# One kernel in two stages on one Trainium2 core: a written order table in place of a list scheduler

## The chip, the cores and the metric

The kernel runs on one core of a Trainium2 chip. A core has five engines with instruction streams of their own: TensorE (PE, matmuls; its weight loads are counted as PEld), VectorE (DVE), ScalarE (ACT), GpSimd (POOL) and SyncE (SP), which here issues nearly all DMA transfers. They wait for one another by semaphores. The metric is the time of one execution on the device in microseconds (us), lower is better; the time before is the median of three runs. The profile's span, from the first to the last instruction, is a little shorter than that time.

## The reference

Two stages follow each other. The first is a gated linear attention of 4 batches, 8 heads, 768 steps and head size 48. The second is a gated MLP with a spatial product over the 768 steps (width 384, inner width 1024).

```python
for t in range(S):
    state = alpha[:, :, t, :, None] * state + np.einsum('bhd,bhe->bhde', k[:, :, t], v[:, :, t])
    y[:, :, t] = np.einsum('bhd,bhde->bhe', q[:, :, t], state)
# x = y with the heads side by side: (4, 768, 384)
h = np.maximum(x @ w_in, 0.0)
u, v = h[..., :512], h[..., 512:]
v_n = (v - mean(v)) / np.sqrt(var(v) + 1e-06)          # over the 512
v_s = np.einsum('ts,bsd->btd', w_spatial, v_n) + b_spatial[None, :, None]
out = (u * v_s) @ w_out
```

## The kernel before

The recurrence is done in 24 chunks of 128 steps (6 for each batch). Of a chunk the kernel forms running sums of log alpha by a matmul (`cum`), scales k by exp(-sum) and q by exp(sum) (`kt`, `qt`), transposes both on TensorE (`trk` or `tr`) and copies them out (`ev`), forms masked scores (`sc`, then `m` with a mask) and from them and the state of the chunk before the output (`y`). The state is carried on by `upd` (matmul), `z` (add), `S` (scale) and `sb` (a bf16 copy). Then `y` is copied and transposed (`xs`, `xt`, `xe`) into x. The first six chunks go as three pairs, in which each partition holds two neighbouring steps, so that the pieces of a load are twice as long (384 bytes); their operations have a p in the name (`cump`, `ktp`). The second stage has for each batch six groups of `v` with statistics (`bn`, `rs`, `vn`), eight of `u`, eight of the spatial product `s` with its bias and gate (`g`), and six of the output product `o` with its store (`st`).

Each operation is recorded with its engine or engines, a length in us, what it depends on, and a function that emits it. Nothing is emitted where it is recorded:

```python
class Op:
    def __init__(self, eng, dur, emit, deps=(), prio=0.0, take=None, lat=0.13, cols=0): ...
# ... (cut)
def dma(key, us, emit, deps, prio, eng="SP", issue=0.99, lat=1.9):
    o = op(key + ("issue",), eng, issue, emit, deps, prio=prio)
    return op(key, "DMA", us, lambda _: None, [o], prio=prio, lat=lat)
# ... (cut)
op(("cump", j, par), "PE", 0.33 + 0.1, cum, got(("lnp", j)), prio=P + 2, take=sl_c[par], cols=768)
op(("ktp", j, par), {"POOL": 0.9, "DVE": 0.6}, None, ktf, got(("einvp", j, par), ("kc", 2 * j)) + tr_users("k", jo), prio=P + 4)
```

A list scheduler then runs through the recorded operations while the program is built. It takes the operation that can start first on its engine in a model of time (lengths as given, a load lands 1.9 us or, for single chunks, 3.5 us after its modelled transfer), bent by tables of patience by kind and of nudges for single operations. Where TensorE would wait in the model before 40 us, it puts in junk matmuls, which write a buffer that is not yet in use:

```python
for eng, dur in op.eng.items():
    start = max(ready, free.get(eng, 0.0))
    key = (round(start + (0.5 * dur if len(op.eng) > 1 else 0.0) + op.wait + ..., 2), ...)
    if best is None or key < best[0]:
        best = (key, n, eng, start, dur)
# ... (cut)
if op.take and start < warm_to:            # junk, warm_from 2.0, warm_to 40.0
    # ... (cut) as many junk matmuls of 96 to 384 columns as fit before start
    fill.append(cols)
# ... (cut)
op.emit(eng)
```

Other rules are that a weight load follows a named load of q, k or v (`late`), and that the stores of the first 11 output tiles follow the last loads. The finished program is a fixed stream for each engine; what an engine waits for at run time is found from the data.

Of the kernel before, what the change touches and what calls it, by code (L numbers as in the profile page):

```python
# [16 lines left out]
class Op:  # L17


    def __init__(self, eng, dur, emit, deps=(), prio=0.0, take=None, lat=0.13, cols=0):  # L20
        self.eng = {eng: dur} if isinstance(eng, str) else dict(eng)
        self.emit, self.prio, self.lat, self.cols = emit, prio, lat, cols
        self.take = [take] if isinstance(take, Slot) else list(take or ())
        self.deps = [d for d in deps if d is not None]
        assert not any(isinstance(d, list) for d in self.deps)
        self.end = None
        self.wait = 0.0
        self.big = False


class Ring:


    def __init__(self, bufs):
        self.bufs, self.taken = bufs, []

    def free_at(self, k):

        n = len(self.taken) - self.bufs + k
        if n < 0:  # L40
            return 0.0
        users = self.taken[n].users
        if any(u.end is None for u in users):
            return None
        return max([u.end + u.lat for u in users], default=0.0)
# [7 lines left out]
class Clock:  # L53


    TICK, ENOUGH = 3.4133, 3100.0

    def __init__(self):
        self.count = {}

    def warm(self, t):
        return self.count.get(int(t / self.TICK) - 1, 0.0) >= self.ENOUGH

    def run(self, t, dur, cols):

        end = t + dur * (1.0 if self.warm(t) else 2.0)
        x = t
        while x < end - 1e-9:
            k = int(x / self.TICK + 1e-9)
            y = min(end, (k + 1) * self.TICK)  # L70
            self.count[k] = self.count.get(k, 0.0) + cols * (y - x) / (end - t)
            x = y
        return end


PATIENCE = {"ev": -0.3, "kt": -0.2, "be": 0.2, "sb": -0.1, "bb": 0.3, "ln": 0.2, "z": -0.1, "S": 0.1, "o": 0.2, "cast": -0.1, "rs": 0.1, "trk": -0.1, "xs": -0.3, "xe": -0.2, "y": -0.2, "eexp": -0.3}
# [11 lines left out]
NUDGE = {  # L88
    ("vn", 0, 4): -0.3,
    ("v", 0, 5): 0.6,  # L90
    ("vbp", 0, 0): -0.6,
    ("ev", "q", 1, 1): 0.15,
    ("cast", "w_in", 0, 1): -0.15,
    ("vb", 21): -0.15,
    ("o", 3, 2, "mm", 0): 0.3,
    ("sc", 1, 0): -0.3,
    ("tr", "k", 0, 1): -0.3,
    ("y", 2): 0.15,
    ("ebc", 2): 0.6,
    ("sb", 4): 0.3,  # L100
    ("m", 1, 1, 0): -0.3,
    ("tr", "k", 1, 0): -0.6,
    ("einv", 17): 0.15,
    ("st", 2, 1): 1,
    ("eexp", 10): -0.3,
    ("wt", 5): -0.15,
    ("cast", "w_out", 3): -0.15,
    ("cump", 0, 0): 1,
    ("ev", "q", 0, 1): -0.6,
    ("ln", 7): 0.6,  # L110
    ("cump", 0, 1): 1,
    ("ev", "q", 1, 0): -0.3,
    ("v", 0, 1, "mm", 0): 0.3,
    ("kc", 2): -0.15,
    ("cast", "w_in", 1, 0): 0.6,
    ("wt", 2): -0.15,
    ("u", 0, 3, 1): 1,
    ("ebc", 1): -0.6,
    ("cast", "w_in", 0, 0): -0.15,
    ("eexpp", 1, 1): 0.15,  # L120
    ("st", 1, 4): 1,
    ("cast", "w_in", 0, 2): 0.3,
    ("xt", 3): 0.15,
    ("z", 1): -0.6,
    ("u", 3, 0, 0): -0.3,
    ("lnp", 0): 1,
    ("xs", 7): 0.3,
    ("y", 0): -0.3,
    ("u", 3, 1, 0): -1.5,
}  # L130
PAIRS = (0, 1, 2)
LATE = 3.5
BETWEEN = 0.06
ACT_STATS = ((2, 2), (1, 4))
PIECES = {
    "w_in": ((0, "vc", 1, 0.35), (0, "kc", 2, 0.15)),
    "w_sp": ((0, "vc", 4, 0.35), (0, "qc", 6, 0.25), (0, "qc", 6, 0.25)),
    "w_out": (0, "vc", 7, 0.35),
}


def schedule(ops, fill, warm_from, warm_to):

    free = {}
    clock = Clock()
    small = 0.0
    todo = list(ops)
    while todo:
        best = None
        for n, op in enumerate(todo):  # L150
            if any(d.end is None for d in op.deps):
                continue
            ready = max([d.end + d.lat for d in op.deps], default=0.0)
            waits = [slot.ring.free_at(k) for k, slot in enumerate(op.take)]
            if None in waits:
                continue
            ready = max([ready] + waits)
            for eng, dur in op.eng.items():
                start = max(ready, free.get(eng, 0.0))
                key = (round(start + (0.5 * dur if len(op.eng) > 1 else 0.0) + op.wait + (small if eng == "PE" and not op.big and start < free.get("PE", 0.0) + 0.05 else 0.0), 2),  # L160
                       ready if eng == "DMA" else op.prio)
                if best is None or key < best[0]:
                    best = (key, n, eng, start, dur)
        assert best is not None, "nothing can start"
        _, n, eng, start, dur = best
        op = todo.pop(n)
        if eng == "PE":
            if op.take and start < warm_to:
                t = max([free.get(eng, 0.0), warm_from] + [slot.ring.free_at(k) for k, slot in enumerate(op.take)])
                while True:  # L170
                    each = 0.00042 if clock.warm(t) else 0.00084
                    cols = min(384, int((start - t) / each) // 32 * 32)
                    if cols < 96:
                        break
                    fill.append(cols)
                    t = clock.run(t, 0.00042 * cols, cols)
            end = clock.run(start, dur + (0.0 if op.big or start > free.get(eng, 0.0) + 0.05 else small), op.cols)
            small = 0.0 if op.big else BETWEEN
        else:
            end = start + dur  # L180
        for slot in op.take:
            slot.ring.taken.append(slot)
        free[eng] = end
        op.end = end
        op.emit(eng)


@with_exitstack
def kernel(
# [14 lines left out]
    B, H, S, D = q.shape  # L204
# [11 lines left out]
    N = B * NCH  # L216
    WARM = 40.0
# [4 lines left out]
    WK = 3  # L222
    NB, NKP = 3, 2
    LD, LP, WT, ST = 1.03, 1.46, 2.35, 0.8
# [116 lines left out]
    def op(key, *args, **kw):  # L341

        users = kw.pop("use", ())
        o = Op(*args, **kw)
        for s in users:
            s.users.append(o)
        ops.append(o)
        made[key] = o
        o.wait = PATIENCE.get(key[0], 0.0) + NUDGE.get(key, 0.0)
        return o  # L350

    def got(*keys):
        return [made.get(x) for x in keys]
# [42 lines left out]
    def finish_x(i):  # L396
# [20 lines left out]
        def xe(eng):  # L417
            if c == 0:
                tiles(b)
# [20 lines left out]
    def pair(j):  # L440
# [33 lines left out]
        for par in range(2):  # L474
# [45 lines left out]
            op(("ktp", j, par), {"POOL": 0.9, "DVE": 0.6}, None, ktf, got(("einvp", j, par), ("kc", 2 * j)) + tr_users("k", jo), prio=P + 4)  # L520
# [7 lines left out]
            op(("qtp", j, par), "DVE", 0.47, qtf, got(("eexpp", j, par), ("qc", 2 * j)) + tr_users("q", jo), prio=P + 4, use=[sl_c[par]])  # L528
# [111 lines left out]
    def first(i):  # L640
# [16 lines left out]
        dma(("ac", i), LD, load("ac", alpha), io_users("ln", j), P, lat=LATE)  # L657
        dma(("kc", i), LD, load("kc", k), io_users("kt", j), P + 0.1, lat=LATE)
        dma(("qc", i), LD, load("qc", q), io_users("qt", j), P + 0.2, lat=LATE)
        dma(("vc", i), LD, load("vc", v), io_users("vb", j), P + 0.3, lat=LATE)  # L660

# [104 lines left out]
        for s, sl in ((0, sl0), (1, sl1)):  # L766
            op(("m", i, s), "DVE", 0.6, mk(s), got(("sc", i), ("y", i - WK)), prio=P + 7.5, use=[sl])
# [77 lines left out]
    def bias():  # L845
        for th in range(2):
# [9 lines left out]
            op(("bb", th), "PE", 0.2, emit, got(("b_sp",)), prio=50.0, take=sl)  # L856
# [4 lines left out]
    def second_v(b, tt):  # L861
# [51 lines left out]
        op(("rs", b, t0), "ACT", 0.45, rs, got(("bn", b, t0), ("bn", b, tt), ("mv", b, t0)), prio=6.0)  # L913
# [82 lines left out]
    def second_o(b, tt):  # L996
# [31 lines left out]
        if n < KEEP:  # L1028
            late.extend((made[("st", b, tt, "issue")], (x, N - 1, "issue")) for x in ("ac", "kc", "qc", "vc"))
# [9 lines left out]
        (("w_in", half), PIECES["w_in"][1 - half], w_in_sb[half],  # L1039
         moe_w_in.rearrange("(ks p) f -> p ks f", p=128)[:, :, half * DH:half * DH + DH]) for half in (1, 0)]  # L1040
    pieces += [
        (("w_sp", n), PIECES["w_sp"][n], None,
         moe_w_spatial.rearrange("(tt p) s -> p tt s", p=128)[:, 2 * n:2 * n + 2, :]) for n in range(3)]
    pieces += [(("w_out",), PIECES["w_out"], w_out_sb, moe_w_out.rearrange("(ds p) m -> p ds m", p=128))]
    late, fetched, casts = [], [], []

    def fetch(key, after, to, src):
# [9 lines left out]
        dma(key, WT, load, list(fetched[-NRAW] if len(fetched) >= NRAW else []), 10.0 * after[2] + after[3], issue=0.68)  # L1057
        late.append((made[key + ("issue",)], after[1:3] + ("issue",)))
        for j in range(n):
            tt = 2 * key[-1] + j if to is None else None  # L1060

            def cast(eng, j=j, tt=tt):
# [5 lines left out]
               None, cast, got(key), prio=10.0 * after[2] + 12)  # L1068
# [8 lines left out]
    late.append((made[("b_sp", "issue")], ("vc", 0)))  # L1077
# [22 lines left out]
    for o, after in late:  # L1100
        o.deps += got(after)
    for o, tt in casts:
        o.deps += [made[("wt", tt - NROW)]] if tt >= NROW else []
    schedule(ops, fill, 2.0, WARM)
# [30 lines left out]
```

## Time and profile before

| | |
|---|---|
| time, median of 3 runs | 154.69 us (154.53 to 154.72) |
| span of the profile | 152.9 us |
| ScalarE busy | 108.7 us |
| GpSimd busy | 86.0 us |
| HBM read, written | 23.60 MB, 4.72 MB |
| mean granted TensorE clock | 0.995 of full |

The page gives busy time and share of the span for each engine, and the span in 40 equal slices with a digit for the busy tenths of each. Its groups of instructions name a line of the kernel, engine, operation and tiles (out<-in); a line may be that of a helper, as L826 for all matmuls of the second stage and L249 for junk. The chain of waits follows the end of the program back to what released each step. A timeline row has the start, the length, engine, line, operation, tiles and shapes, and in brackets the idle time before it and what ended it. Ends of matmuls are modelled and overlap the next one, so that the distance of starts tells more of TensorE's pace than the length of a row.

### The profile page before, as it was taken

How to read it: one execution, taken by the hardware profiler on the slowest of the kernel's cores; microseconds unless marked ns; L12 is line 12 of the kernel's file. 1: busy time of each engine (PE TensorE's matmuls, PEld its weight loads, DVE VectorE, ACT ScalarE, POOL GpSimd, SP SyncE). 2: the span in 40 equal slices, each digit the busy share in tenths (PEclk: the TensorE clock that was granted, in tenths of full speed). 3: DMA queues.
4: the chain of work that ended last, by engine and by line, in shares of the span. 5: the costliest groups of instructions: out<-in, count | busy, mean ns of one | idle time of the engine just before them, and what ended most of it. 6: DMA issues, size and time to landing. Idle time of an engine off the chain costs nothing.

```text
span 152.9 us, 4478 instructions
## 1 busy us (share of the span) xinstructions
PE 145.2 (95%) x1713; PEld 90.3 (59%) x1713; DVE 121.6 (80%) x260; ACT 108.7 (71%) x268; POOL 86.0 (56%) x151
## 2 busy tenths in 40 slices
PE   6899999799999999999999999999999999999990
PEld 3366756467566666466657556666666565656550
DVE  7888598797899899878799889689789867566820
ACT  3566677697697975899984598998956778880050
POOL 6847356462249698814369987242699873003620
PEclk9999999999999999999999999999999999999998
DMA  4999999799899997998998999999980131230044
GB/s 123 266 313 290 316 242 273 200 285 210 155 296 174 249 205 154 204 221 164 211 209 174 202 190 194 212 184 202 303 322 9 51 107 51 100 110 0 0 157 154
DMA packets 93013, 28.60 MB, mean 187 GB/s; under 512 B 87872, under 2 KB 91456, under 8 KB 92992
## 3 DMA queue, kind: packets, MB, share of 16 engines
q1 hardware_dynamic: 92960, 28.32, 78.9%
q8 instruction: 13, 0.21, 0.6%
q14 instruction: 8, 0.07, 0.2%
q0 software_dynamic: 32, 0.00, 0.0%
HBM read 23.60 MB, written 4.72 MB: 185 GB/s over the span
## 4 chain that ended last, share of the span: by engine, by line
PE 88%; ACT 3%; DVE 3%; DMA 2%; issue 1%; DVEq 0%; ACTq 0%
PE ps L826 52%; PE pt L722 5%; PE pt L752 4%; PE y L413 3%; DMA ac<-in_alpha_dram 2%; PE y L780 2%; PE cum L671 2%; PE tp L738 2%; PE y L623 2%; PE y L774 2%; PE y L249 2%; PE ps L545 2%; PE ps L480 1%; PE ps L836 1%; PE ps L249 1%; PE tp L576 1%
## 5 line engine op out<-in xcount | busy, mean ns | idle before, releaser
L826 PE MATMUL ps<-w_spT,vn 128*128 128x384 bf16 x192 | 37.2, 326 | 0.0
L979 POOL TENSOR_TENSOR gT<-vsb,uT 128x384 bf16<-128x384 f32 x29 | 26.3, 926 | 14.7 <-DVE vsb L966 14.7
L763 DVE TENSOR_TENSOR ptm<-pt,mask 128x512 bf16<-128x512 f32 x36 | 23.3, 680 | 3.2 <-PE pt L752 3.1
L695 POOL TENSOR_TENSOR kt<-kc,binv 128x384 bf16<-128x384 f32 x18 | 16.4, 913 | 12.0 <-ACT binv L683 10.5
L384 POOL TENSOR_TENSOR state<-state,bc 128x192 f32<-128x192 f32 x20 | 10.2, 509 | 22.8 <-DVE state L379 11.6
L826 PEld LDWEIGHTS <-vn 128*128 128x128 bf16 x192 | 16.4, 97 | 8.9 <-issue 0.2
L826 PE MATMUL ps<-w_in,xT 128*128 128x512 bf16 x72 | 19.5, 380 | 0.0
L826 PE MATMUL ps<-xT,w_in 128*128 128x384 bf16 x96 | 18.9, 326 | 0.0
L826 PE MATMUL ps<-w_out_sb,gT 128*128 128x384 bf16 x96 | 18.8, 327 | 0.0
L966 DVE TENSOR_TENSOR vsb<-ps,bsp_bc 128x384 f32<-128x384 f32 x31 | 16.4, 552 | 2.9 <-PE ps L826 2.9
L257 ACT CAST x_sb<-y 128x384 bf16<-128x384 f32 x24 | 11.5, 478 | 9.2 <-PE y L780 5.8
L888 DVE BATCH_NORM_STATS2 stats<-v_sb 128x6 f32<-128x512 bf16 x20 | 13.8, 688 | 2.4 <-ACT v_sb L263 2.3
L263 ACT ACTIVATE v_sb<-ps 128x512 bf16<-128x512 f32 x20 | 11.9, 597 | 3.3 <-PE ps L826 3.1
L259 POOL CAST sbd<-state 64x192 bf16<-64x192 f32 x38 | 13.0, 343 | 1.7
L683 ACT ACTIVATE binv<-cum 128x384 bf16<-128x384 f32 x18 | 8.8, 491 | 6.3 <-PE cum L674 5.7
L259 DVE COPY kqT<-pt 128x1024 bf16<-128x1024 bf16 x15 | 10.3, 690 | 3.3 <-PE pt L722 3.0
L257 ACT COPY xT<-y 128x384 bf16<-128x384 bf16 x24 | 11.4, 480 | 1.8 <-PE y L413 1.4
L263 ACT ACTIVATE uT<-ps 128x384 bf16<-128x384 f32 x24 | 11.2, 492 | 1.0 <-PE ps L826 1.0
L826 PEld LDWEIGHTS <-w_in 128*128 128x128 bf16 x96 | 8.3, 97 | 5.3
L826 PEld LDWEIGHTS <-gT 128*128 128x128 bf16 x96 | 8.4, 98 | 4.9
L918 DVE TENSOR_SCALAR vn<-v_sb,mvs,rstd 128x512 bf16<-128x512 bf16 x24 | 10.3, 467 | 1.1 <-ACT rstd L911 1.1
L257 ACT COPY o_sb<-ps 128x384 f32<-128x384 f32 x9 | 4.3, 481 | 9.1 <-PE ps L826 9.1
(129 smaller groups left out, 296.7 us busy)
## 6 DMA issues: line engine op xcount, KB each, us to landing
ac<-in_alpha_dram SPq DMA_DIRECT2D x18, 192.0 KB, 4.2
kc<-in_k_dram SPq DMA_DIRECT2D x18, 192.0 KB, 4.1
qc<-in_q_dram SPq DMA_DIRECT2D x18, 192.0 KB, 3.8
vc<-in_v_dram SPq DMA_DIRECT2D x18, 192.0 KB, 4.0
raw_w<-in_moe_w_spatial_dram SPq DMA_DIRECT2D x3, 768.0 KB, 5.5
out_dram<-raw_w SPq DMA_DIRECT2D x12, 192.0 KB, 3.1
out_dram<-o_sb SPq DMA_DIRECT2D x9, 192.0 KB, 1.9
raw_w<-in_moe_w_in_dram SPq DMA_DIRECT2D x2, 768.0 KB, 8.1
```

Source lines behind the costliest of these rows:

```text
L257: nc.scalar.copy(out=out, in_=in_)
L259: ENG[eng].tensor_copy(out=out, in_=in_)
L263: nc.scalar.activation(out=out, in_=in_, func=AF.Relu)
L384: ENG[eng].tensor_tensor(out=st["state"], in0=st["state"], in1=st["bc"][:, :, None].to_broadcast([128, HP, D]), op=ALU.mult)
L683: nc.scalar.activation(out=st["binv"], in_=st["cv"], func=AF.Exp, scale=-1.0)
L695: ENG[eng].tensor_mul(out=kt[:, :, :, 0:D], in0=quad(st["kc"]), in1=st["binv"])
L763: nc.vector.tensor_tensor(out=st["ptm"][:, s], in0=st[f"pt{s}"], in1=mask4, op=ALU.mult)
L826: return lambda ps: nc.tensor.matmul(out=out(ps), lhsT=lhsT(), rhs=rhs(), start=start, stop=stop)
L888: nc.vector.bn_stats(out=stats, in_=d["v_sb"][:, tt, :])
L918: nc.vector.tensor_scalar(out=d["vn"][:, t, :], in0=d["v_sb"][:, t, :], scalar1=d["mvs"][:, t, 0:1], scalar2=d["rstd"][:, t:t + 1], op0=AL ...
L966: nc.vector.tensor_tensor(out=hold["vs"], in0=ps[:, 0:TH], in1=bsp_bc[:, th, :], op=ALU.add)
L979: ENG[eng].tensor_tensor(out=bt[b]["gT"][:, dsl, cols], in0=hold["vs"], in1=bt[b]["uT"][:, dsl, cols], op=ALU.mult)
```

## The change

The scheduler, the tables of patience and nudges, the model of the clock and the rules for weight loads and stores go. In their place stands a table with one word for each of the 1108 operations, in the order of emission: a letter for the engine (P TensorE, D VectorE, A ScalarE, G GpSimd, S SyncE, Q the transfer itself), the number of the operation as recorded, and for TensorE the columns of junk matmuls ahead of it. Its purpose is an order that was planned outside the kernel, with the times at which loads really arrived in two traces, and with junk that keeps TensorE going until the first sums.

```diff
-def schedule(ops, fill, warm_from, warm_to):
-    ... (cut: the list scheduler)
+PLAN = """
+G32 Q33 G0 S34 S36 Q35 S38 S96 S40 Q37 S98 D1 S100 S166 A42 Q39 S102 D2 S170
+P43:384:384:384:384:384:384:384:384:384:384:384:384 S168 G3 Q97 S4 P54:384 A46 A44 S172 A45 S303 G47 A57 A55 D48 Q41
+S9 A56 D58 P50:384:384:384:384:384:384:384:96 P52 A51 D59 P61:128 Q99 D53 A62 P63:256 D64 A104 P245:384 P243 P73
+... (cut: 47 more lines of this kind)
+"""
+def replay(ops, fill, plan):
+    for word in plan.split():
+        number, *junk = word[1:].split(":")
+        op, eng = ops[int(number)], LETTERS[word[0]]
+        assert eng in op.eng and not op.done and all(d.done for d in op.deps), op.key
+        fill.extend(int(x) for x in junk)
+        op.emit(eng)
+        op.done = True
...
-    schedule(ops, fill, 2.0, WARM)
+    replay(ops, fill, PLAN)
```

In the first lines G32 is the load of b_sp, G0 the constants, S34, S36, S38 and S40 the loads of log-decay, k, q and v of the first pair, P43 and P54 its two running sums, and P50 its first transposes; S4 and S9 are the two halves of w_in. Where the engine of an operation is free, the table chooses too; this moves some operations:

| operation | engine | before | table |
|---|---|---|---|
| u | VectorE, ScalarE | 8, 24 | 14, 18 |
| ev | VectorE, ScalarE | 26, 4 | 21, 9 |
| ktp | VectorE, GpSimd | 3, 3 | 1, 5 |
| casts of weights | VectorE, ScalarE, GpSimd | 2, 6, 8 | 6, 3, 7 |

Single copies of other kinds (be, sb, g, we, vb, vbp) move by one or two. The matmuls of the two stages are the same in number and shape. Stores stand among the last loads in SyncE's stream. Some dependencies on constants (`cz`) that followed from the model's order before are now written out.

## The prediction

> **What bounds the kernel now.** I read the page first, then busy time by stretches of 10 us, then the chain of waits, then TensorE's timeline, and last the issue and landing of each load. The page:
>
> ```profile
> span 152.9 us, 4478 instructions
> ...
> PE 145.2 (95%) x1713; PEld 90.3 (59%) x1713; DVE 121.6 (80%) x260; ACT 108.7 (71%) x268; POOL 86.0 (56%) x151
> ...
> PE   6899999799999999999999999999999999999990
> ...
> DMA  4999999799899997998998999999980131230044
> ```
>
> TensorE is busy in every slice, and the DMA engines until slice 29 (110 us). But busy TensorE includes junk matmuls, which fill waits to keep the clock up. The stretches of junk alone (columns: length, PE busy, PEld busy, DVE busy, clock, DMA share, GB/s):
>
> ```profile
> 5.48:10.00 4.52, 1.93 (x11) 0.91 (x12) 0.00 (x0) 1.00 1.27 268
> 10.00:20.00 10.00, 4.00 (x24) 1.87 (x22) 0.00 (x0) 1.00 1.16 308
> 20.00:30.00 10.00, 1.89 (x13) 0.99 (x13) 0.00 (x0) 1.00 0.98 249
> 30.00:40.00 10.00, 1.26 (x6) 0.55 (x6) 0.00 (x0) 1.00 0.91 211
> ```
>
> So the slack lies before 40 us. After that TensorE does real work only. The chain of waits, its start and its end:
>
> ```profile
> 0.74 3.76 DMA ac<-in_alpha_dram
> 4.59 0.85 ACT la L469
> 5.48 0.48 PE ps L480 x2
> ...
> 13.69 1.79 PE y L249 x11
> ...
> 133.40 15.43 PE ps L826 x92
> 148.85 0.48 ACT raw_w L257
> ```
>
> The first sums start at 5.48 us, after a load and a logarithm which the change leaves as they are. The last matmul ends at 133.40+15.43 = 148.83, and 152.9-148.83 = 4.1 us of copy and store follow. Eleven junk matmuls of 384 columns take 1.79 us, so 0.163 us each, 0.42 ns a column.
>
> How long is the real work? From TensorE's timeline I take how far the start of one operation lies from the start of the next where nothing is awaited: three matmuls of the spatial product, here 42.78 to 43.26, 0.487 us.
>
> ```profile
> 42.78 0.65 PE L826 MATMUL ps<-w_spT,vn 128*128 128x384 bf16 x3
> 43.26 0.36 PE L780 MATMUL y<-vb,ptm 128*128 128x48 bf16 x8
> 43.47 0.65 PE L826 MATMUL ps<-w_spT,vn 128*128 128x384 bf16 x3
> 43.95 0.39 PE L722 MATMUL pt<-ident,kt 128*128 128x128 bf16 x4
> ```
>
> In the same way for all: 64 spatial halves x 0.487 = 31.2; 24 o x 0.650, 24 v x 0.648 and 32 u x 0.487 = 46.8; 18 trk x 0.445 = 8.0; sc 18 x 0.329 + 6 x 0.350 = 8.0; y 10.2 and upd 4.9; cum and cump 8.3; 24 xt x 0.168 = 4.0; 12 tr, 6 wt and 2 bb 5.0. Sum 126.4 us. The path from 5.48 to 148.83 is 143.35 us. Junk after the first sums is 52 matmuls of 15,872 columns, x 0.42 ns = 6.7 us. So 143.35-126.4-6.7 = 10.3 us are waits: 4.6 before 40 us (1.3 open gaps, 3.3 in operations that start late by up to 0.9), and 5.6 us after, some 0.5 us in every 10, in slips mostly below 0.1 us.
>
> [...] the junk's weight loads from 1.62 to 4.50 stand 0.32 us apart, and the two sums from 5.48 stand 0.16 apart, after 3.7 us of junk. [...]
>
> **The change part by part.** (1) Real work is not changed: both programs hold 1649 real matmuls with 295,012 columns. Junk falls from 64 matmuls to 38, 20,416 to 12,032 columns. Before the first sums it stays (4,544 columns become 4,608), so the clock should be up by 5.48 again. After them 26 remain, 7,424 columns x 0.42 = 3.1 us. If nothing waits, TensorE ends at 5.48+126.4+3.1 = 135.0 instead of 148.8.
>
> (2) Loads. All loads of the three pairs but one come before the weights. The one queue delivers in the order of issue here; from the landings in the trace a pair load takes 1.5 us (ac 4.50, kc 6.00, qc 7.51, vc 9.00), a single load 0.8, a weight load 2.1 to 3.4, and I take 2.6. That gives in the new order: ac of pair 1 at 9.0, vc of pair 0 at 10.5, kc and qc of pair 1 at 12.0 and 13.5, ac of pair 2 at 15.0, vc of pair 1 at 16.5, qc and kc of pair 2 at 18.0 and 19.5, the first half of w_in at 22.1, vc of pair 2 at 23.6, the second half of w_in at 27.0, w_sp at 29.6, 33.8 and 38.8. Against this I set when an unhindered TensorE wants each, which is 5.48 us plus all real work and junk ahead of the operation in the new order:
> - the second state update of batch 0's second pair (upd 2) wants vc of pair 1 plus two casts of 0.5 at 16.8 and has it at 17.5: 0.7 late;
> - the first v wants w_in plus a cast of 0.6 (three engines share it) at 21.2 and has it at 22.8: 1.6 late in all;
> - the first u wants the other half at 25.8, which is 27.4 with the delay so far, and has it at 27.9 after casts: 2.1 late in all.
> After this w_sp (wanted at 30.9, there at 30.5), kc of 6 and the later loads come in time, with more room towards the end, because 24 stores of about 0.5 us are spread among and after them. Loads add 2.1 us.
>
> (3) Start of the chain. ktp of the first pair goes from VectorE (0.84) to GpSimd (0.91), while its mask work ends at 7.22. Issuing the load of b_sp, now first on GpSimd, takes 0.67 us, and lies in a 0.72 us wait for VectorE's lt_pair. The first transposes start near 8.25 instead of 7.69, as the junk ahead of them (2784 columns, 1.2 us) has it anyway. In the first 20 us ScalarE's chain (extra ebc ahead of einv, ev on ScalarE at 0.60 instead of 0.42) adds about 0.6, and I leave 0.9 for slips between 20 and 40. Together 1.5.
>
> (4) From 40 us on the small slips come from switching between short and long operations and from waits of a few ns, and the table switches as often. I keep all 5.6 us.
>
> (5) VectorE. The change puts 6 u, 4 casts, one be, one sb and one g on it and takes away 5 ev, 2 ktp and one we, about +2 us of work. What it has to do in the first 60 us of real matmul time is about 63 us by the durations of its rows, and less time will be there for it. The chain of waits already ran over VectorE from 58.8 to 60.4 in the kernel before. I give it no term of its own in the middle, and room in the range.
>
> Sum: 135.0+2.1+1.5+5.6 = 144.2 for the last matmul, +4.1 of tail = 148.3 of span, +1.8 (154.69 of the clock against 152.9 of span before) = 150.1 us, 3.0% less.
>
> **The rivals.** (a) The loads are the bound, and the junk only filled their waits: then gaps take its place, and the gain is small. For it: the DMA share of 0.9 to 1.2 in all stretches to 110 us. Against it: the same bytes in a better order, and the last load landed at 109.8 us while the first transposes that use it ran after 118. In the first 40 us it is half true, and 2.1 us are counted. If each weight load takes 3.4 us, 0.8 more on each of the five, the start loses 2 to 3 us more: 152.5. (b) VectorE becomes the bound between 20 and 70 us; it was 9.88 busy of 10 in the stretch 50 to 60. For it the +2 us and the shorter time; against it, its idle time before 40 us (3.0, 1.6 and 1.6 us in the three stretches from 10 to 40). It would cost 1 to 2 us: 151.5. (c) The table was made from traces, so it also removes a part of the slips, say half: 147.3. (d) The table is tuned so closely that each late load holds an engine, and the delays add up over its dependencies; stores now stand among the last loads in one queue, and a late store holds the loads behind. This could eat all: 154 to 156. Against it: every engine's order shifts together, and loads have room after 45 us by the times above.
>
> **Range and chances.** 150.0 us. 147.2 to 152.6 holds half of the slips removed on one side, and slow weights or VectorE on the other. Faster by over 2% means below 151.6: 0.78. Within 2%: 0.19. Slower by over 2%, above 157.8, takes (d) at its worst: 0.03.
>
> **What would show it.** Right: first sums at about 5.5 with two sums 0.16 apart; the first v near 23 instead of 18.1, waiting for w_in; real work in every stretch from 30 us on and junk nowhere after; the closing run of L826 products, which starts at 133.4 before, starting near 127, and the last matmul near 144. Wrong: sums still at half clock; gaps ended by DMA beyond 45 us; VectorE above 9.5 of 10 in several stretches with TensorE waiting for ptm, kqT or vsb; idle SyncE waits for stores that hold loads.

## The result and the profile after

The kernel with the order table takes 148.88 us (median of 4 runs, 148.50 to 149.26), the kernel before 154.70 us beside it (154.53 to 156.12). The ratio is 0.960, with a 95% interval of 0.955 to 0.966: 3.4 to 4.5% less. The prediction said 150.0 us, within 147.2 to 152.6.

The same lines of the page, now of the changed kernel (instructions, busy time of each engine, then TensorE's and the DMA engines' busy tenths in 40 slices):

```profile
span 147.5 us, 4398 instructions
...
PE 140.0 (95%) x1687; PEld 89.8 (61%) x1687; DVE 121.9 (83%) x266; ACT 105.6 (72%) x264; POOL 87.1 (59%) x149
...
PE   6899999989998999999999999999999999999990
...
DMA  4999999989999899899996999997949302250154
```

TensorE's share is 95% as before, which by itself says nothing: 5.2 us of its busy time went. The stretches of junk alone (columns: length, PE busy, PEld busy, DVE busy, clock, DMA share, GB/s) say where from:

```profile
5.41:10.00 4.59, 2.40 (x12) 1.09 (x12) 0.00 (x0) 1.00 1.29 261
10.00:20.00 10.00, 1.54 (x9) 0.75 (x9) 0.00 (x0) 1.00 1.18 252
20.00:30.00 10.00, 1.22 (x6) 0.46 (x6) 0.00 (x0) 1.00 1.06 302
30.00:40.00 10.00, 0.00 (x0) 0.00 (x0) 0.00 (x0) 1.00 1.02 261
```

Junk ends before 30 us, and the clock stays at 1.00 without the rest of it. The first two sums, in TensorE's timeline, start at 5.41 and stand 0.16 us apart, so the clock was up (by the trace's record of it, from 4.27 us on):

```profile
5.41 0.32 PE L413 MATMUL ps<-la,le_pair 128*128 128x384 bf16 x1 [0.53 <-ACT la L402]
5.57 0.32 PE L413 MATMUL ps<-la,lt_pair 128*128 128x384 bf16 x1
```

The chain of waits of the changed kernel (start, length, what; line numbers have moved, L759 is the helper that was L826):

```profile
0.63 0.59 issue
1.26 0.62 issue
1.88 0.24 POOL le_pair L225
...
7.63 0.90 POOL kt L449
8.57 0.62 PE ps L478 x8
...
19.52 8.84 DMA raw_w<-in_moe_w_in_dram
28.38 1.19 DVE w_in L193 x2
...
126.67 17.12 PE ps L759 x103
143.82 0.33 ACT raw_w L191
```

Three things are to be seen. At its start the chain no longer runs over the first load and logarithm, but over GpSimd: b_sp's issue, the masks, ktp, and at 8.57 the first transposes. In the middle there is one load, the second half of w_in. At the end the closing run of second-stage products starts at 126.67 instead of 133.40, and the last matmul ends at 143.8 instead of 148.8.

To add up as the prediction did, I take for each TensorE operation the distance from its start to the next start, less the length it has undisturbed in the kernel before, and less 0.42 ns for each column of junk. What is left is waiting.

| us | before | predicted | after |
|---|---|---|---|
| first sums start | 5.48 | 5.48 | 5.41 |
| real matmuls | 126.4 | 126.4 | 126.4 |
| junk after the first sums | 6.7 | 3.1 | 3.1 |
| waits up to 40 us | 4.6 | 3.6 | 5.0 |
| waits after 40 us | 5.6 | 5.6 | 3.9 |
| last matmul ends | 148.8 | 144.2 | 143.8 |
| copy and store | 4.1 | 4.1 | 3.7 |
| span | 152.9 | 148.3 | 147.5 |

The changed kernel's columns add up, but two of the terms are off in opposite directions. So the question for the experiments was less whether the table is faster than what in it is: the start, the rest of the order, the order of the loads, or the junk.

### The profile page after: what moved, and what is told of

Its sections match the earlier page's. It is cut to its first block, busy times and chain, and to the rows that moved or that the text cites. A ratio compares the mean times of both kernels' runs of the same rounds, so it can differ in the third digit from the quotient of the medians.

```text
span 147.5 us, 4398 instructions
## 1 busy us (share of the span) xinstructions
PE 140.0 (95%) x1687; PEld 89.8 (61%) x1687; DVE 121.9 (83%) x266; ACT 105.6 (72%) x264; POOL 87.1 (59%) x149
## 4 chain that ended last, share of the span: by engine, by line
PE 79%; DMA 6%; POOL 4%; ACT 3%; DVE 3%; issue 3%; SPq 0%; POOLq 0%
PE ps L759 51%; DMA raw_w<-in_moe_w_in_dram 6%; PE pt L655 6%; PE pt L685 4%; PE tp L671 2%; PE y L346 2%; PE y L713 2%; PE cum L604 2%; POOL mask L243 2%; PE y L707 2%; PE ps L478 1%; PE ps L769 1%; PE ps L413 1%; PE ps L183 1%; ACT xT L191 1%
## 5 line engine op out<-in xcount | busy, mean ns | idle before, releaser
L759 PE MATMUL ps<-w_spT,vn 128*128 128x384 bf16 x192 | 36.2, 326 | 0.0
L912 POOL TENSOR_TENSOR gT<-vsb,uT 128x384 bf16<-128x384 f32 x28 | 25.6, 925 | 15.7 <-DVE vsb L899 15.1
L696 DVE TENSOR_TENSOR ptm<-pt,mask 128x512 bf16<-128x512 f32 x36 | 23.8, 681 | 0.3 <-PE pt L685 0.2
L759 PEld LDWEIGHTS <-vn 128*128 128x128 bf16 x192 | 17.0, 97 | 9.7 <-issue 0.2
L759 PE MATMUL ps<-xT,w_in 128*128 128x384 bf16 x96 | 19.7, 326 | 0.6 <-ACT xT L191 0.4
L899 DVE TENSOR_TENSOR vsb<-ps,bsp_bc 128x384 f32<-128x384 f32 x31 | 16.5, 550 | 3.6 <-PE ps L759 3.2
L759 PE MATMUL ps<-w_in,xT 128*128 128x512 bf16 x72 | 19.5, 379 | 0.0
L759 PE MATMUL ps<-w_out_sb,gT 128*128 128x384 bf16 x96 | 18.4, 326 | 0.0
L193 POOL CAST sbd<-state 64x192 bf16<-64x192 f32 x36 | 12.3, 342 | 1.5
L759 PEld LDWEIGHTS <-w_in 128*128 128x128 bf16 x96 | 8.6, 97 | 6.6 <-issue 1.1
L759 PEld LDWEIGHTS <-gT 128*128 128x128 bf16 x96 | 8.9, 98 | 5.7
L638 DVE TENSOR_TENSOR qt<-qc,cum 128x384 bf16<-128x384 f32 x18 | 9.9, 549 | 2.3 <-ACT cum L633 2.0
L193 DVE COPY kqT<-pt 128x1024 bf16<-128x1024 bf16 x14 | 9.6, 687 | 2.3 <-PE pt L655 2.2
L851 DVE TENSOR_SCALAR vn<-v_sb,mvs,rstd 128x512 bf16<-128x512 bf16 x24 | 9.6, 428 | 0.2 <-ACT rstd L844 0.2
```

Of the source, the lines that this page charges most:

```text
L193: ENG[eng].tensor_copy(out=out, in_=in_)
L638: nc.vector.tensor_mul(out=qt[:, :, :, 0:D], in0=quad(st["qc"]), in1=st["cv"])
L696: nc.vector.tensor_tensor(out=st["ptm"][:, s], in0=st[f"pt{s}"], in1=mask4, op=ALU.mult)
L759: return lambda ps: nc.tensor.matmul(out=out(ps), lhsT=lhsT(), rhs=rhs(), start=start, stop=stop)
L851: nc.vector.tensor_scalar(out=d["vn"][:, t, :], in0=d["v_sb"][:, t, :], scalar1=d["mvs"][:, t, 0:1], scalar2=d["rstd"][:, t:t + 1], op0=AL ...
L899: nc.vector.tensor_tensor(out=hold["vs"], in0=ps[:, 0:TH], in1=bsp_bc[:, th, :], op=ALU.add)
```

## The experiments

My theory: the start up to 40 us is worth some 3 to 4 us, because less junk runs there and loads come in a better order, and the rest of the order removes slips, about 2 us. One rival is that the parts cannot be had singly, because each part of the order expects buffers and operands in the state in which the part ahead of it leaves them. The other is that the loads bound the start and neither order nor junk counts. The order of the kernel before can be written as a table too, so that two orders can be joined at a seam. That this changes nothing in itself is seen in e6, whose first part is such a table: it ends at 68.50 us, in the kernel before at 68.56. One thing no run separates: the table's order and its changed choice of engines (14 of the u on VectorE instead of 8, and so on). Below, "order" means both.

| run | what | us, median | ratio to before | 95% interval |
|---|---|---|---|---|
| e1 | table to 39 us, then the old order | 155.69 | 1.003 | 1.001 to 1.006 |
| e2 | old order to 40 us, then the table | 152.72 | 0.987 | 0.986 to 0.989 |
| e3 | table, old order of the first 25 loads | 159.03 | 1.028 | 1.026 to 1.030 |
| e4 | old order, new order of those loads | 165.96 | 1.072 | 1.069 to 1.076 |
| e5 | table for the first 125 TensorE operations, then old | 154.21 | 0.994 | 0.992 to 0.997 |
| e6 | old for the first 125, then the table | 152.18 | 0.983 | 0.978 to 0.988 |
| e7 | table without junk after the first sums | 154.81 | none given | |
| e8 | table without junk before the first sums | 150.07 | 0.969 | 0.965 to 0.973 |
| e9 | table, stores behind all loads | 149.37 | 0.966 | 0.964 to 0.969 |
| e10 | table, b_sp issued later | 149.89 | 0.968 | 0.967 to 0.970 |
| e11 | e10 and one swap on VectorE | 151.13 | 0.968 | 0.966 to 0.969 |
| e12 | table, load of ac 6 later, and that swap | 149.20 | 0.965 | 0.963 to 0.967 |

In e1, e5, e10 and e11 a part of the executions took some per cent longer than the rest (in e11 three of six, in e10 one of five, these with a lower clock); the medians count them, the ratios leave them out. For e7 no ratio was formed.

### The start alone (e1) and the rest alone (e2)

```diff
 # e1, TensorE's words at the seam (the other engines likewise)
  P321 P255 P247
- P251 P344 P248 P256 P328        the table goes on
+ P344 P328 P251 P351 P330        what is left, in the order of the kernel before
 # e2
  P237 P217 P321
- P223 P325 P225 P344 P227        the order of the kernel before goes on
+ P227 P225 P223 P229 P325        what is left, in the table's order
```

> The table's order up to the first half of the spatial product (39 us in its trace), then the order of the kernel before for all that is left. By real matmul work done at 40 us (26.6 us against 23.3) the start is worth 3.3 us, the rest of the gain (about 2 us) comes from fewer small slips after 40 us. Theory 'start and slips': about 151.4 us. Rival 'the start is all': 148.9 to 149.5 us. Rival 'the whole table is needed, a seam costs as much as the start brings': 153 us or more.

> The order of the kernel before up to the state update of chunk 6 (40 us in its trace), then the table's order for all that is left. Theory 'start and slips': 148.9 + 3.3 = about 152.2 us. Rival 'the start is all': 154 to 155 us. Rival 'the slips are most of it': 150 to 151 us.

e1 took 155.69 us by the median, 1 us more than the kernel before (0.3% more by the ratio), as the third theory of its expectation had it, and its 20 executions scattered from 153.87 to 159.74. Its profile (span 154.5, an execution of 156.31 us) has the table's start whole: at 40 us 26.6 us of real matmuls are done, as in the changed kernel, where the kernel before has 23.3. Then 3.5 and 2.3 us of waits come in the next two stretches of 10 us, where the kernel before has 0.3 and 0.4. Two rows of e1's timeline for TensorE:

```profile
42.90 0.40 PE L654 MATMUL pt<-ident,kt 128*128 128x128 bf16 x4 [1.00 <-POOL kt L627]
...
56.42 0.40 PE L654 MATMUL pt<-ident,kt 128*128 128x128 bf16 x4 [1.50 <-POOL kt L627]
```

The transposes stand open for 1.0 and 1.5 us, each time for GpSimd's kt. In this execution what was won at the start is waited away at once. The old order has these transposes where kt was in time for a TensorE that came 3 us later; that this is why is argued from the rows, not tried. After 60 us the waits are the old ones, 4.8 us. e2 took 152.72 us, 0.5 more than expected; from 60 us on its waits are 2.0 to 2.5 us, those of the table.

So the rival with the seam holds for the start, and my sum of parts does not: the start alone is worth nothing, the rest alone 1.9 us, and both 5.8. Of these 5.8, 3.8 come when the new start goes before the new rest (152.72 to 148.88).

### A later seam (e5, e6)

The seam at 40 us cuts the recurrence with the loads still coming. After the first 125 operations of TensorE, up to the first products of o, both orders have done the same set: at 68.6 us in the kernel before and at 65.6 in the changed one. That is a cleaner place to join them.

```diff
 # e5, TensorE's words at the seam
  P581 P283 P497
- P295 P291 P499 P588 P299        the table goes on
+ P291 P588 P499 P590 P295        what is left, in the order of the kernel before
 # e6
  P474 P287 P497
- P291 P588 P499 P590 P295        the order of the kernel before goes on
+ P295 P291 P499 P588 P299        what is left, in the table's order
```

> As the first seam, but laid where both orders have done exactly the same 125 operations on TensorE (the output product of the second tile of batch 0 is the last; 65.6 us in the table's trace, 68.6 in that of before). First part by the table, rest by the order before. By the two traces the first part is worth 2.9 us and the rest 2.4. Theory 'both parts pay by themselves, the loss at the first seam was the seam': 151.5 to 152.2 us. Rival 'the start's gain is given back by the old order anyway': 154 us or more.

> The other way round, with the seam at the same set: the order before for the first 125 operations of TensorE, then the table. Theory 'both parts pay by themselves': 151.8 to 152.4 us. Rival 'slips belong to the chip, not to the order' (my prediction's term of 5.6 us): 153.8 to 154.6 us.

e6 came as expected at 152.18 us. From the seam to the end of the last matmul it takes 78.2 us, where the kernel before takes 80.3 for the same operations after the same first part. So those slips belong to the order and not to the chip. e5 did not come as my theory had it, but as the rival did. It took 154.21 us, with 20 executions from 152.73 to 157.71, though the clock was 0.994 or more in 17 of them. In its profile the waits between 60 and 70 us are 1.9 us, half of them in the first transposes behind the seam, which wait for GpSimd's kt as in e1:

```profile
68.72 0.40 PE L655 MATMUL pt<-ident,kt 128*128 128x128 bf16 x4 [0.93 <-POOL kt L628]
```

The set of finished TensorE operations was equal there, but how far GpSimd was ahead need not have been, and an order written for one lead need not fit another. This reading is argued from the row as in e1. Why e1 and e5 scatter so much more than the orders that were planned whole stays open.

### The order of the loads alone (e3, e4)

```diff
 # e3, SyncE's words (e4 is the reverse, in the old order)
- S34 S36 S38 S96 S40 S98 S100 S166 S102 S170 S168 S4 S172 S303 S9 ...
+ S34 S36 S38 S40 S96 S4 S98 S100 S9 S102 S166 S168 S170 S172 S303 ...
```

S4 and S9 are the halves of w_in, S166 is ac of pair 2.

> The table, with only the first 25 loads put back into the order of the kernel before (w_in sixth and ninth, as early as before). TensorE, VectorE, ScalarE and GpSimd keep the table's order. Theory 'the order of loads and of work only pays together': q, k and v of pairs 1 and 2 come 2.6 to 5.5 us later while w_in lies unused, the loss is not made up later: 153 to 155 us. Rival 'the loads are hidden, the engines' order is what pays': 149 to 150.5 us.

> The order of the kernel before written as a table, with only the first 25 loads in the new order. TensorE wants w_in for the first v at 18.1 us, and it lands at 23.1. Theory 'only together': a wait of about 5 us at the first v, of which up to 2 us come back because pair 2 is there sooner: 157 to 160 us. Rival 'the new load order is the gain by itself': 150 to 152 us.

Both cost more than any theory had: 159.03 and 165.96 us. In e3 TensorE waits for the log of the late ac of pair 2 (first fence: its timeline), and then its clock halves (second fence: stretches, the columns are length, PE, PEld, DVE, ACT and POOL busy, clock, DMA share, GB/s):

```profile
22.58 0.48 PE L413 MATMUL ps<-la,le_pair 128*128 128x384 bf16 x1 [4.16 <-ACT la L402]
```

```profile
18.00:22.00 4.00, 0.42 (x18) 0.35 (x17) 1.44 (x3) 0.32 (x1) 0.95 (x2) 0.72 1.03 230
22.00:26.00 4.00, 3.42 (x50) 2.08 (x50) 1.04 (x3) 2.70 (x7) 0.51 (x1) 0.50 0.91 220
26.00:30.00 4.00, 4.00 (x52) 2.90 (x51) 2.15 (x5) 1.36 (x4) 3.78 (x8) 0.50 0.01 2
30.00:34.00 4.00, 4.00 (x50) 2.72 (x49) 2.47 (x5) 2.32 (x6) 1.63 (x3) 0.50 0.35 94
34.00:38.00 4.00, 3.67 (x48) 1.77 (x47) 2.00 (x4) 1.56 (x5) 0.27 (x1) 0.65 0.77 204
```

The wait is 4.2 us, but the loss is 10 us: TensorE works at 0.50 for another 14 us after it, although it is busy nearly throughout from 22.6 us on. The DMA engines then stand idle too (0.01 of their time from 26 to 30 us). The waits of SyncE between 16 and 36 us (sum, times, longest) say why: the load of w_sp waits for the buffer that VectorE's cast of w_in frees, and all loads behind it in the stream wait with it.

```profile
SPq L986 <- DVE w_in L193: 8.3, 1, 8.3
```

In the trace's record of the granted clock the fall comes at 19.75 us, 1.3 us into the wait; in the 3.41 us ahead of that TensorE was busy for 2.08. The return comes at 36.82, 14.2 us after TensorE was at work again, and in these it was busy for 13.89:

```profile
16.34:19.75 3.41, 2.08 (x51) 1.70 (x50) 3.06 (x8) 1.01 (x2) 1.06 (x3) 1.00 1.18 272
22.58:36.80 14.22, 13.89 (x174) 8.85 (x176) 6.96 (x14) 7.33 (x17) 5.92 (x11) 0.50 0.52 133
```

In e4 VectorE stands idle for 8.5 us until w_in lands, casts it at 22.67, and only then, as the order has it, makes the masked scores (ptm) that the first y wants, at 23.02. TensorE waits 7.1 us for them, and the clock is 0.50 from 21.9 to 28.7 us (here the fall comes 5 us into the wait):

```profile
22.67 0.43 DVE L194 CAST w_in<-raw_w 128x512 bf16<-128x512 f32 x1 [8.49 <-DMA raw_w<-in_moe_w_in_dram]
23.02 1.28 DVE L541 TENSOR_TENSOR ptm<-pt,mask 128x512 bf16<-128x512 f32 x2
```

An old order with new loads, or a new one with old loads, is worse than either: the load order pays only with the order of the work.

### Junk (e7, e8)

```diff
 # e7: the columns go from all words behind P43, 26 junk matmuls in all
- P54:384 ... P50:384:384:384:384:384:384:384:96 ... P61:128 ...
+ P54 ... P50 ... P61 ...
 # e8: the columns go from P43, the first sums, alone
- P43:384:384:384:384:384:384:384:384:384:384:384:384
+ P43
```

> The table without the 26 junk matmuls after the first sums (3.1 us of TensorE time); the 12 ahead of them stay. Theory 'junk lies only in waits': gaps take its place, the clock stays up[...], 148.4 to 149.3 us. Rival 'junk is in the way of real work': 146.5 to 148 us. Rival 'without it the clock falls in the start': 151 us or more, with a clock under 0.98.

> The table without the 12 junk matmuls ahead of the first sums; the 26 after them stay. [...] Theory 'the loads bound the start': 1 to 1.5 us late at 10 us, half of it taken up by the waits for loads at 10 to 18 us: 149.2 to 150.2 us. Rival 'nothing is caught up': 150.5 to 152 us. Rival 'warming up is worth nothing': 148.6 to 149.1 us.

e7 took 154.81 us, as the rival had it by which the clock falls. The 3.1 us of junk that it lacks came back as 5.9 us of time. Of its 20 executions 19 took 153.94 to 155.34 us at mean clocks of 0.917 to 0.933, and the best, 151.00 us at 0.966, is still longer than any of the changed kernel. Its stretches (columns as above):

```profile
10.00:20.00 10.00, 9.89 (x154) 6.62 (x155) 6.51 (x15) 5.99 (x14) 5.26 (x10) 0.50 1.22 258
20.00:30.00 10.00, 10.00 (x156) 6.91 (x153) 7.10 (x14) 5.48 (x13) 5.76 (x11) 0.50 0.72 205
```

TensorE seems busier than ever, and is at half clock from 7.4 to 31.3 us. So the junk after the first sums is not filling that may go: without it the clock held in none of the 20 executions (means of 0.917 to 0.966). e8 took 150.07 us, within what was expected if loads bound the start. In its profile the clock comes up only at 9.80; the first two sums start 0.27 us apart instead of 0.16, and the first transposes at 9.95 instead of 8.57; about 0.7 us less real work is done at 10 us, and the span ends 0.5 us later (148.0 against 147.5). The twelve junk matmuls ahead of the first sums are worth 0.5 us by the spans and 1.2 us by the medians. Nor do they always work: in e2, e3, e6, e9 and e10 the first sums started at 5.3 to 5.6 us and ran 0.33 us long with all twelve in place. In the 13 profiles with all twelve the clock comes up anywhere from 4.00 to 7.21 us; what sets the moment was not shown. The changed kernel's own profile (4.27) happened to have the switch in time.

### Stores behind the loads (e9)

```diff
 # SyncE
- ... S753 S847 S877 S875 S908 S297 S281 S948 S912 S879 S301 S910 ...
+ ... S753 S847 S877 S875 S908 S948 S912 S879 S910 ...      (all 24 stores after the last load)
```

> The new table, with all stores of results moved behind the last load in the order of the load engine. Rival (d) says that stores which stand among the last loads and wait for their results hold loads back: then the time falls by 0.5 us or more, to 148.4 or less. My theory is that no load is needed soon enough to be held by them: 148.9 us, 0.4 either way, the same as the new table.

149.37 us, and the ratio's interval (0.964 to 0.969) overlaps that of the changed kernel (0.955 to 0.966). In the profile TensorE's busy time is alike to about 0.1 us in every stretch of 10 us from 30 us on. Stores among the last loads hold nothing that matters. Rival (d) of the prediction had no part in this.

### The start on GpSimd, a swap, and a load (e10, e11, e12)

```diff
 # e10: GpSimd issues b_sp (G32) behind ktp (G47)
- G32 G0 G3 G47 G49
+ G0 G3 G47 G32 G49
 # its broadcast on TensorE (P245, P243) goes ahead of upd 2 (P127), and 384 + 288 columns of junk go
- P63:256 P245:384 P243 P73 ... P85 P127:288
+ P63:256 P73 ... P85 P245 P243 P127
 # e11: e10, and qt 7 (D349) ahead of the bias sum of s (D253)
- D257 D24 D253 D349
+ D257 D24 D349 D253
 # e12: the table with that swap, the load of ac 6 (S303) behind w_in (S9), its sums (P312) later
- S172 S303 S9 ... P206 P312 P90 ... P158 P210
+ S172 S9 S303 ... P206 P90 ... P158 P312 P210
```

> The new table, with GpSimd's issue of the b_sp load moved from the first place behind the first transposes' operand (ktp of chunk 0), and the operations that use b_sp moved back to fit. If the issue costs the start what the chain of waits shows, GpSimd's masks are ready 0.4 us or more sooner, the first transposes start at 8.2 us or before instead of 8.57, and the time falls by up to 0.4 us, to 148.5. If the loads set the start anyhow (as the run without the first junk showed), the transposes come sooner and the time stays at 148.9.

> The same as the run with the late b_sp issue, and one swap more: VectorE makes qt of step 7 ahead of the sum for the spatial product's second block, for which TensorE's transposes waited 0.57 us at 44 us. If this wait is one of the slips that add up, the time is 0.5 us below that of the run without the swap; if the next wait takes its place, since VectorE is 90% busy or more there, it is the same within 0.2 us.

> The new table with the load of ac 6 (3.4 us ahead of the second half of w_in on the one queue, 0.56 us of its time) moved behind that half, the log and the sums that use ac 6 moved behind the first two u products to fit, and VectorE's qt of step 7 ahead of the sum for the spatial product's second block. All junk matmuls stay. If the loads bound the start, the second half of w_in lands 0.5 us sooner (27.9 us), the first u product starts near 29.1 us instead of 29.61, and with the swap the last matmul ends 0.5 to 0.8 us sooner: 148.2 us, 0.4 either way. If the waits just move on to the next load or engine, as in the runs with the late b_sp issue, it stays at 148.9 to 149.4.

In e10 the GpSimd part came out as the chain said. First the changed kernel's GpSimd timeline, then that of e10:

```profile
1.22 0.67 POOL L1006 DMA_DIRECT2D b_sp_sb<-in_moe_b_spatial_dram  x1 [0.78 <-POOLq L1046]
1.88 0.23 POOL L225 MEMSET le_pair<- 128x128 bf16 x1
...
7.61 0.91 POOL L449 TENSOR_TENSOR kt<-kc,binvp 128x384 bf16<-128x384 f32 x1
```

```profile
0.73 0.21 POOL L225 MEMSET le_pair<- 128x128 bf16 x1 [0.29 <-POOLq L1046]
...
2.23 0.29 POOL L231 TENSOR_SCALAR_AFFINE_SELECT lt_pair<-lt_pair 128x128 bf16<-128x128 bf16 x1 [0.72 <-DVE lt_pair L229]
...
7.21 0.91 POOL L449 TENSOR_TENSOR kt<-kc,binvp 128x384 bf16<-128x384 f32 x1
```

The issue as the first work of GpSimd puts the first mask off by 1.15 us (1.88 against 0.73). Of this 0.72 lies in the wait for VectorE's lt_pair, and 0.4 stays: ktp starts at 7.61 instead of 7.21. Yet the time did not fall; it rose, by the ratio from 0.960 to 0.968, and the intervals do not overlap. In e10's profile the first sums ran long and hid the gain. In that of e11, which has the same start, they did not: the transposes begin at 8.18, as expected, and the scores after them at 10.10 instead of 10.46:

```profile
8.18 0.40 PE L478 MATMUL ps<-ident,kt 128*128 128x128 bf16 x4
...
10.10 0.42 PE L529 MATMUL pt<-kqT 48*64 48x128 bf16 x16 [0.52 <-DVE kqT L193]
```

But TensorE now stands open for 0.5 us ahead of the scores, where the broadcast of b_sp (0.4 us) had lain. The broadcast had filled a wait; put later, it takes time of its own, and at upd 2, which still waits for vc of pair 1, TensorE is at 18.5 us as in the changed kernel (18.4). I had also taken away two groups of junk with it, 672 columns or 0.28 us. With both changes the clock was no longer safe: it fell in three of the six executions of e11 and in one of the five of e10 (means of 0.961 to 0.966, and 0.934), and in none of the four of the changed kernel. No run separates the later broadcast from the junk. The profile of e11 shows the clock fallen from 18.8 to 29.0 us:

```profile
20.00:30.00 10.00, 9.84 (x133) 6.72 (x127) 5.78 (x12) 4.57 (x10) 5.81 (x11) 0.55 0.89 281
```

Here nothing stood open for long: no TensorE operation before that started more than 0.75 us late. Such short waits do not settle it, since in the other half of the executions of the same order the clock held (means of 0.997 to 0.999).

The swap came from two VectorE rows of the changed kernel:

```profile
43.75 0.55 DVE L899 TENSOR_TENSOR vsb<-ps,bsp_bc 128x384 f32<-128x384 f32 x1
44.21 0.54 DVE L638 TENSOR_TENSOR qt<-qc,cum 128x384 bf16<-128x384 f32 x1
```

The transposes (trk 7) wait for qt, which VectorE starts at 44.21, after vsb (43.75); they run 0.57 us late. With the swap this wait is gone, and 0.32 us of it comes back at once before the first v of batch 1. The ratio of e11 is within 0.001 of that of e10, so the swap is worth nothing that the runs resolve.

In e12 the second half of w_in landed at 26.90 instead of 28.36, more than the 0.56 us that I had moved away, and the first u products started at 29.29 instead of 29.61:

```profile
29.29 1.14 PE L759 MATMUL ps<-xT,w_in 128*128 128x384 bf16 x6
```

Of 1.46 us of earlier landing, 0.32 reached TensorE, and as much the last matmul of the profile (143.46 against 143.78). VectorE, which casts w_in, was then not ready: the last step of its statistics started at 28.08, and the cast came next, at 28.18; in the changed kernel it started at 28.38. So the load that the chain of waits names is only 0.2 to 0.3 us ahead of the next bound there. The median is 149.20 us, not the 148.2 of my first theory but what the second one gave, and the ratio's interval (0.963 to 0.967) overlaps that of the changed kernel. I found no version that beats the changed kernel beyond what its measurement resolves.

## Why the prediction was right, point by point

**Sum without waits (1).** 135.0 us predicted; 5.41 + 126.4 + 3.1 = 134.9 measured. Right. That the clock would be up at the first sums was in part luck: it came too late for them in the profiles of five other runs with the same junk ahead. That the junk which stays would hold the clock was taken for granted, and e7, e10 and e11 show how near the edge this is: with none of it the gain is gone.

**Loads and the start (2, 3).** The term was too small: 2.1 + 1.5 = 3.6 us of waits predicted up to 40 us, 5.0 measured. The order of landings was right, the times slid from one load on:

| load | predicted | landed |
|---|---|---|
| vc of pair 0, kc and qc of pair 1, ac of pair 2 | 10.5, 12.0, 13.5, 15.0 | 10.5, 12.0, 13.5, 15.0 |
| vc of pair 1 | 16.5 | 17.8 |
| first half of w_in | 22.1 | 23.1 |
| second half of w_in | 27.0 | 28.4 |
| w_sp, three blocks | 29.6, 33.8, 38.8 | 30.6, 34.5, 40.2 |

A load every 1.5 us held to 15.0. Then vc of pair 1 took 2.9 us, while the data rate stayed at some 250 GB/s. That is 0.7 MB for a load of 0.39 MB, so bytes of other loads moved ahead of its last ones. What came after was about 1 us late throughout. The second state update shows it in the timeline, at 18.4 and 18.9, for the cast of that load:

```profile
17.91 0.29 PE L183 MATMUL tp<-junk 128*128 128x192 bf16 x2
18.43 0.18 PE L509 MATMUL tp<-vbp,kt 64*64 64x48 bf16 x1 [0.23 <-POOL vbp L193]
18.87 0.43 PE L509 MATMUL tp<-vbp,kt 64*64 64x48 bf16 x15 [0.27 <-POOL vbp L193]
```

The first v started at 24.28 ("near 23"), the first u at 29.61 (27.9). Part of that is the load and part the casts that queue on VectorE and ScalarE (e12), and the split between them is not settled.

**GpSimd (3).** That b_sp's issue "lies in a 0.72 us wait" was wrong by 0.4 us: I counted its 0.67 but not the idle time ahead of it, 1.15 together. The transposes started at 8.57, not 8.25. By e11 this is made up by upd 2, before 20 us.

**Slips after 40 us (4).** "I keep all 5.6 us" was wrong: 3.9 remain, and from 60 us on 2.2 against 4.9. Rival (c) was right about them, though its half was a guess. e6 shows that it is the order. Between 40 and 60 us the table has more waits than before, 1.7 against 0.7; what it wins comes later.

**VectorE (5).** No term, and nearly rightly: 9.5, 9.3 and 9.3 of 10 in the three stretches from 40 to 70 us, with two open waits of TensorE for it, 0.40 for qt at 44.8 and 0.17 for kqT at 54.3. They are a part of the 1.7 us above:

```profile
40.00:50.00 10.00, 9.60 (x107) 6.25 (x106) 9.54 (x19) 7.23 (x17) 5.61 (x9) 1.00 0.97 189
50.00:60.00 10.00, 9.83 (x138) 6.61 (x135) 9.31 (x19) 7.95 (x21) 8.27 (x13) 1.00 1.04 231
60.00:70.00 10.00, 10.00 (x126) 6.63 (x125) 9.25 (x23) 9.57 (x28) 5.42 (x10) 1.00 0.93 182
```

Here the columns after the length are PE, PEld, DVE, ACT and POOL busy. "Became the bound" (rival b) would need several such waits.

**Tail.** 4.1 kept, 3.7 measured. The runs with the table's last part (e2, e6) have 3.7 too, those with the old last part (e1, e5) 4.05, so it goes with the order.

The total fell within 1.1 us because terms cancel: the span missed by +1.4 us for the start, -1.7 for the slips and -0.4 for the tail, with the last 0.1 in the first sums; the other 0.3 us is that the profiled execution (149.26) was longer than the median. So the main term, less junk ahead of the same real work, was right, and that the total came so near was partly luck.

What the prediction did not see is how the gain hangs together. It added a start and left the rest as it was; e1 comes near to that very kernel, and it is no faster than the one before. The mechanism that I named (less junk, and loads in the order of use) is real, but it only reaches the end because the order behind it was written for that start.

## What to carry to other kernels

An order planned whole has to be judged whole: half of it, or its loads without its work, cost up to 11 us here (e4), though neither half is bad in itself. Junk matmuls that bridge short waits are to be taken out only with the granted clock in view, stretch by stretch, since 3.1 us less of them cost 5.9 (e7), and 0.28 us less, together with a broadcast moved, cost 3 us in half of the executions (e11). And the load that a chain of waits names is a bound only up to the next one: before moving it, look what its consumer was doing just before it began (e12: 1.46 us of earlier landing gave 0.32).

## What the runs showed of the hardware that I had not expected

- The clock fell without a full stop. In the profile of e11 TensorE was late by at most 0.75 us at a time and still ran at half clock from 18.8 to 29.0 us. In e3 one wait of 4.2 us was followed by 14.2 us at half clock, in which TensorE was busy for 13.89. So dense busy time in the profile did not bring it back at once; what did is not settled.
- The stretches between changes of the clock had lengths in whole ratios. By the traces' record of it the stretches at half clock last 6.83 us in e4, 10.24 in e11, 17.07 in e3 and 23.89 in e7, and the stretches at full clock ahead of them 17.07, 13.65, 13.65 and 3.41. All eight are whole multiples of 3.41 us (2, 3, 5 and 7; 5, 4, 4 and 1). In these four profiles a clock once lost stayed lost for 6.83 us or more.
- The same twelve junk matmuls had the clock up at the first sums in the profile of the changed kernel and not in those of e2, e3, e6, e9 and e10. The difference is about 0.33 us at the first sums.
- In the profile of the changed kernel the loads of the one queue landed 1.5 us apart in the order of issue up to 15.0 us. Then one came 1.3 us late, with the data rate still at 245 to 268 GB/s, while bytes of other loads went ahead of its last ones (vc of pair 1: 2.9 us after the load ahead of it, the next one 1.4 us after it).
